# Bank layout, weight casts, squares and a rank step around the last attention pairs of a fused attention and expert kernel

## The chip, the cores and the metric

The kernel runs on one core of one Trainium2 chip. The metric is the device time of one execution in microseconds (us), the median of the runs shown. One execution was also recorded by the hardware profiler, and all rows come from it. PE is TensorE, PEld its weight load, ACT ScalarE, DVE VectorE, POOL GpSimd, SP SyncE.

## What is computed

A block-causal attention over 8 batches of 8 heads, 576 positions and 64 columns a head, followed by a mixture of experts on its output, where each token goes to the one expert that its normalised row fits best. Cut to its core, the reference reads:

```python
scores = np.where(mask, scale * q @ k.T, -1e9)           # mask: block_i >= block_j, blocks of 64
attn = np.exp(scores - scores.max(-1, keepdims=True))
x = attn / (attn.sum(-1, keepdims=True) + 1e-9) @ v      # (8, 8, 576, 64) -> 4608 rows of 512
xn, en = x / (norm(x) + 1e-6), emb / (norm(emb) + 1e-6)
logits = xn @ en.T / tau                                 # 8 experts
e = logits.argmax(1)
gate = softmax(logits)[arange(4608), e]
out = gate[:, None] * (np.maximum(x @ w1[e], 0) @ w2[e]) # w1: 512 x 1024, w2: 1024 x 512
```

## The kernel before, in words

The 8 batches of 8 heads make 32 pairs of heads, four pairs to a batch, numbered 0 to 31. Each pair goes through generators: prep, maxes, `scores` (L405; matmuls L422, exponentials on ScalarE L429 and L431 into pT and pA, adds on GpSimd L401 and L403 into pS), `values` (L441; matmuls L457, copies into oe L463), `sums` (L468; matmuls L476, L486, L493 to L500, copy into su L502) and `finish` (L514), which turns su and oe round on TensorE (L326), divides on VectorE into the token rows xrow (L532 to L545), and ends with the squares of the pair's columns on ScalarE (`parts_squares`, L562, one L582 of 128 columns for each of five row tiles). For pair 30 alone the squares aren't done there but put in a list `late`, which the tail runs.

Behind the last pair of a batch comes `route` (L587): the expert of each token on VectorE (L594 to L607), its rank among the tokens of that expert by matmuls (L616, L619, L620), the squares of whole rows (L582, 512 columns), the norm on GpSimd (L648, L651), the place of each token in a table (`table_rows`, L740: a product on GpSimd L745, then VectorE L747 to L752), the gate (L655 to L663), and five indirect DMAs of GpSimd that scatter the token numbers into the table (L672). In the same queue of slow steps stands `early_rows` with `indices` (L690; four small GpSimd operations on enone, L694 to L697), for the rows of two early slots.

The order of all this is written out by hand: one string of letters for each pair (`plan_of`), where s, v, f, m, p, l each run the next piece of scores, values with sums, finish, maxes, prep or loads, k a piece of the router's weights, and r the next piece of the slow queue. The last five pairs have strings of their own in FINAL; FINAL[3] is the string of pair 30, during which the steps of batch 6 go.

Behind the strings stands the tail (from L1240). It reads the token table into tbt (L1243), and starts the expert stage on two early slots of 128 tokens, whose rows ex are at hand before the last batch is routed. A weight of 32 bits is used as a high and a low piece in the rings ring_h (`split_hi`, a cast, L907) and ring_l (`split_lo`, a subtraction, L912); so are the rows, turned round on TensorE (`xt_turn`, L1093) into PSUM and split out of it (`xt_hi` L1097 on ScalarE into xh and hh, `xt_lo` L1101 on VectorE into xl and hl). The first expert layer (`l1`, L1309, by way of `mm3`, matmuls L1122) takes three matmuls for a weight piece and a half of its columns: high by high, low by high, high by low.

PSUM has eight banks. In the attention stage they are four pairs, psm0 (banks 0 and 1) to psm3 (6 and 7), which `take_bank` and `give_bank` hand round in a list. Before the tail the pair `free_bank` (psm2, banks 4 and 5) is taken out for the early rows' turned halves, one bank each. Then three pools take over the eight banks: ps_b (a pair), ps_m1 (four single banks) and ps_e (a pair), in the order in which they are opened; in the kernel before these are banks 0 and 1, 2 to 5, 6 and 7. The main expert stage has a pool `mps` of its own with rotating tiles ph, px, pt and py.

The code that fixes the banks and the casts:

```python
for c in range(NPC):
    split_hi(0, c, 0, eng=nc.gpsimd if c > 1 else nc.scalar)
    if c < 2:
        split_lo(0, c, 0)
load_raw(1, 0, eng=nc.gpsimd)
banks.remove(free_bank)
for u in range(EARLY):
    xt_turn(ea[u], free_bank[:, u])
```

Of the kernel before, what the change touches and what calls it, by code (L numbers as in the profile page):

```python
# [8 lines left out]
F32 = mybir.dt.float32  # L9
# [6 lines left out]
PSUM = bass.MemoryType.PSUM  # L16
# [15 lines left out]
    "rmmvrrvmvvvvrvvspvsrmpsrrrsrvfmvsvrrmrmfflsprrrfvvvrvmmrsfsffrrpvppsspvvppvmvssrrmrmvrvvmmrsmrsrmmsfrfsffssfprrrsmlvfprm",  # L32
    "srvmvpmmrvvrrvmrrrrvrrmppmmrrmvvrrrvvrrrrrmrrrrrrrlp",
    "slrvrrrrmrpsrprrsrsrspsrrrmmssrrrssrrrrrmssmmrmsrfrrfvvrvvrr",
    "rfvfsrrrmrrsmrfvfmrrrrsrrmsvmrvvrrvvrrsrrfrfrvfrrrsfvvfrsvvfvvrvrfrr",
    "rvrrvrrvvlrrrsfrffrrvvsrrrvrvrrrsrrfrsvvfsrfsfffvfrfvrrssrrfffrrrvss",
)

# [10 lines left out]
def kernel(  # L49
# [12 lines left out]
    nc = tc.nc  # L62
# [3 lines left out]
    P = 128  # L66
# [108 lines left out]
    NPAIR = B * NP  # L175
# [6 lines left out]
    def pool(stack, name, bufs, **kw):  # L182
        return stack.enter_context(tc.tile_pool(name=name, bufs=bufs, **kw))
# [10 lines left out]
    psum_t = psum.enter_context(ExitStack())  # L194
    ps_m = pool(psum_t, "ps_m", 1, space=PSUM)
    banks = [ps_m.tile([P, 2, 512], F32, name=f"psm{i}") for i in range(4)]
# [4 lines left out]
    def take_bank():  # L201
        return banks.pop(0) if wide else ps_b.tile([P, 2, 512], F32, name="psb")

    def flat2(t):
        return t.rearrange("p g c -> p (g c)")

    def give_bank(t):
        if wide:
            banks.append(t)
# [114 lines left out]
    def halves_turned(out, a):  # L324
        for g in range(2):
            nc.tensor.transpose(out(g), a[hd[g]], ident[hd[g], hd[g]])  # L326
# [187 lines left out]
    def finish(n, xrow, rin, lgh, ssp):  # L514

        hp = n % NP
        tb = take_bank()
        pt = flat2(tb)

        yield "pe"  # L520
        u0, u1 = NJ * 64, NJ * 64 + 64
        for u in range(2):
            halves_turned(lambda g: pt[:, g * 512 + u0 + u * 64:g * 512 + u0 + u * 64 + 64], su[n % 2][:, u * P:(u + 1) * P])
        yield "fine"
        for j in range(NJ - 1, -1, -1):
            halves_turned(lambda g: pt[:, g * 512 + j * 64:g * 512 + j * 64 + 64], oe[n % len(oe)][:, j * P:(j + 1) * P])
        yield
        r2 = rin[:, :, 2 * hp:2 * hp + 2]
        p2 = pt.rearrange("p (a x) -> p a x", a=2)
        lt = p2[:, :, u0:u1].rearrange("p a (j c) -> p a j c", c=32)  # L530
        c1, c2 = u1 + 32 + 2 * E, 512 + u1 + 2 * E + 1
        nc.vector.tensor_scalar(r2[:, 0:NG].rearrange("p (a j) c -> p a j c", a=2), lt[:, :, :, 2 * E:2 * E + 2],  # L532
                                1.0e-9, None, op0=ALU.add)
        nc.vector.tensor_scalar(r2[:, NG], pt[:, c1:c2 + 1:c2 - c1], 1.0e-9, None, op0=ALU.add)
        nc.vector.reciprocal(r2, r2)
        yield "fine"
        xp = xrow[:, :, hp * P:(hp + 1) * P].rearrange("p j (g d) -> p j g d", d=D)
        nc.vector.tensor_tensor(xp, p2[:, :, 0:u0].rearrange("p g (j d) -> p j g d", d=D),
                                r2.unsqueeze(3).to_broadcast((P, NJ, 2, D)), op=ALU.mult)
        yield  # L540
        for a in range(2):
            nc.vector.tensor_tensor(lgh[:, 2 * a:2 * a + 2, 2 * hp:2 * hp + 2, :],
                                    lt[:, a, :, 0:2 * E].rearrange("p j (g e) -> p j g e", e=E),
                                    r2[:, 2 * a:2 * a + 2].unsqueeze(3).to_broadcast((P, 2, 2, E)), op=ALU.mult)
        nc.vector.tensor_tensor(lgh[:, NG, 2 * hp:2 * hp + 2, :],  # L545
                                pt[:, u1:u1 + 2 * E].rearrange("p (g e) -> p g e", e=E),
                                r2[:, NG].unsqueeze(2).to_broadcast((P, 2, E)), op=ALU.mult)
        give_bank(tb)
        yield
        if n == NPAIR - 2:  # L550
            store(B - 1, xrow, 0, (NP - 1) * P)
        if n >= NPAIR - NP:
            yield "squares"
            if n == NPAIR - 2:
                late.append(lambda: parts_squares(hp, xrow, ssp))
            else:
                parts_squares(hp, xrow, ssp)
            yield

    late = []  # L560

    def parts_squares(hp, xrow, ssp):  # L562
        for j in range(NJ):
            squares(xrow[:, j, hp * P:(hp + 1) * P], ssp[:, j, hp:hp + 1])

    def store(b, xrow, c0, c1):
        r0 = b * S + 1
        nc.sync.dma_start(xbuf[r0:r0 + S - 64, c0:c1].rearrange("(j p) w -> p j w", p=P), xrow[:, 0:NJ - 1, c0:c1])
        nc.sync.dma_start(xbuf[r0 + S - 64:r0 + S, c0:c1], xrow[0:64, NJ - 1, c0:c1])
# [331 lines left out]
    def piece(ring, i, c, half):  # L901
        cs = slice(c * CW, (c + 1) * CW)
        return ring[i][:, half, cs] if isinstance(half, int) else flat(ring[i][:, bass.ds(half, 1), cs])

    def split_hi(i, c, half, to=None, eng=nc.scalar):
        to = i if to is None else to
        return (nc.scalar.copy if eng is nc.scalar else eng.tensor_copy)(  # L907
            piece(ring_h, to, c, half), raw[i][:, c * CW:(c + 1) * CW])

    def split_lo(i, c, half, to=None, eng=nc.vector):  # L910
        to = i if to is None else to
        return eng.tensor_tensor(piece(ring_l, to, c, half), raw[i][:, c * CW:(c + 1) * CW],  # L912
                                       piece(ring_h, to, c, half).bitcast(F32), op=ALU.subtract)
# [104 lines left out]
    def rotate(pool, name, n, shape, dt):  # L1018
        sets[name] = [pool.tile(shape, dt, name=f"{name}{i}") for i in range(n)]
        turn[name] = 0  # L1020
# [234 lines left out]
        slots[g]["w", 0] = half_of(0, 0)  # L1255
        slots[g]["w", 1] = half_of(0, 1)
    for c in range(NPC):
        split_hi(0, c, 0, eng=nc.gpsimd if c > 1 else nc.scalar)
        if c < 2:
            split_lo(0, c, 0)  # L1260
    load_raw(1, 0, eng=nc.gpsimd)
    banks.remove(free_bank)
    for u in range(EARLY):
        xt_turn(ea[u], free_bank[:, u])
    drain(values(NPAIR - 1))
# [4 lines left out]
    split_lo(0, 2, 0)  # L1270
    xt_lo(ea[1], free_bank[:, 1])
    psum_t.close()
    ps_b = pool(psum_t, "ps_b", 1, space=PSUM, reuse_waits="tile")
    ps_m = pool(psum_t, "ps_m1", 4, space=PSUM, reuse_waits="tile")
    wide.clear()
    ps_e = pool(psum_t, "ps_e", 1, space=PSUM, reuse_waits="tile")
    pts = [ps_e.tile([P, 512], F32, name=f"pe{u}") for u in range(2)]
    drain(last_f)
    split_lo(0, 3, 0)
    late.pop()()  # L1280
    for c in range(NPC):
        split_hi(1, c, 1, to=0, eng=nc.gpsimd)
    load_raw(0, 1, (2, 3, 0, 1))
# [103 lines left out]


    mps = ctx.enter_context(tc.tile_pool(name="mps", bufs=1, space=PSUM, reuse_waits="tile"))
    rotate(mps, "py", 1, [P, DM], F32)  # L1390
    rotate(mps, "px", 1, [P, 512], F32)
    rotate(mps, "ph", 2, [P, 512], F32)
    rotate(mps, "pt", 2, [P, 1024], F32)
    NU = NT // P - EARLY

    def turn_pe(g):
# [130 lines left out]
```

## Time and profile before

| what | value |
|---|---|
| runs | 811.25, 808.84, 810.61 us |
| median | 810.61 us |
| the profiled execution | 810.42 us |
| its span, from the first instruction to the last | 808.7 us |
| granted TensorE clock, mean | 1.0 |
| TensorE, busy share of the span | 96% |
| VectorE, GpSimd, ScalarE | 75%, 54%, 50% |
| DMA over the span | 93.95 MB, 116 GB/s |

The attention stage and the change's place end near 363 us; from there on TensorE runs expert matmuls of 512 columns to the end. A timeline row gives the start of an instruction (or of several alike, counted after the x) and its duration in us, engine, line and operation, the tiles written and read, and in brackets how long the engine stood idle ahead of it and what released it. A "q" behind an engine's name is its instruction queue or sequencer.

### The profile page before, as it was taken

How to read it: one execution, taken by the hardware profiler on the slowest of the kernel's cores; microseconds unless marked ns; L12 is line 12 of the kernel's file. 1: busy time of each engine (PE TensorE's matmuls, PEld its weight loads, DVE VectorE, ACT ScalarE, POOL GpSimd, SP SyncE). 2: the span in 40 equal slices, each digit the busy share in tenths (PEclk: the TensorE clock that was granted, in tenths of full speed). 3: DMA queues.
4: the chain of work that ended last, by engine and by line, in shares of the span. 5: the costliest groups of instructions: out<-in, count | busy, mean ns of one | idle time of the engine just before them, and what ended most of it. 6: DMA issues, size and time to landing. Idle time of an engine off the chain costs nothing. (4 is left out here: it accounts for less than half of the span.)

```text
span 808.7 us, 23043 instructions
## 1 busy us (share of the span) xinstructions
PE 779.2 (96%) x7160; PEld 627.3 (78%) x7160; DVE 604.2 (75%) x1382; ACT 408.4 (50%) x831; POOL 435.7 (54%) x420
## 2 busy tenths in 40 slices
PE   8999999999999998899999999999999999999997
PEld 3678878787878776668878887788888888888885
DVE  6667878686868776658868777877887778877881
ACT  2566757575757564664744456553533332543222
POOL 7555676767676757772347288784761111661110
PEclk9999999999999999999999999999999999999999
DMA  4745364545454543163845357454441111111111
GB/s 104 169 95 136 84 158 105 147 104 132 101 140 100 141 100 101 29 231 127 297 151 166 100 158 235 152 167 150 148 153 45 55 54 45 38 49 55 54 35 39
DMA packets 141421, 93.95 MB, mean 116 GB/s; under 512 B 118925, under 2 KB 120541, under 8 KB 141260
## 3 DMA queue, kind: packets, MB, share of 16 engines
q1 hardware_dynamic: 133228, 69.74, 31.2%
q0 software_dynamic: 8032, 22.36, 8.7%
q8 instruction: 66, 1.08, 0.6%
q14 instruction: 95, 0.78, 0.3%
HBM read 72.71 MB, written 19.71 MB: 114 GB/s over the span
## 5 line engine op out<-in xcount | busy, mean ns | idle before, releaser
L1175 DVE STREAM_TRANSPOSE pt<-h 32x256 f32<-32x256 f32 x528 | 240.6, 456 | 31.3 <-ACT h L1149 14.1
L367 DVE TENSOR_REDUCE nmx<-psm 128x16 f32<-128x1024 f32 (+2 forms) x128 | 125.6, 986 | 21.4 <-PE psm L361 18.5
L912 POOL TENSOR_TENSOR ring_l<-raw,ring_h 128x1024 f32 (+1 forms) x49 | 116.3, 2406 | 35.7 <-ACT ring_h L907 20.0
L1189 POOL DMA_INDIRECT out_dram<-y,outi x36 | 36.7, 1020 | 176.5 <-ACTq L1061 118.8
L1122 PE MATMUL py<-ring_h,hh 128*128 x272 | 109.3, 402 | 0.7 <-ACT h L1149 0.7
L1122 PE MATMUL py<-ring_l,hh 128*128 x272 | 106.3, 391 | 0.0
L429 ACT ACTIVATE pT<-psm 128x640 f32<-128x640 f32 (+2 forms) x128 | 89.1, 703 | 28.2 <-PE psm L361 16.8
L403 POOL TENSOR_TENSOR pS<-pS,pT 128x640 f32<-128x640 f32 (+2 forms) x93 | 93.5, 1006 | 10.9 <-ACT pT L431 3.2
L1122 PE MATMUL py<-ring_h,hl 128*128 x272 | 88.8, 389 | 0.0
L1122 PE MATMUL ph<-ring_l,xh 128*128 x280 | 86.3, 390 | 0.8 <-POOLq L1073 0.8
L1122 PE MATMUL ph<-ring_h,xh 128*128 x280 | 86.3, 389 | 0.6 <-ACTq L1061 0.6
L457 PE MATMUL psm<-pT,vo 128*64 128x320 f32 (+2 forms) x640 | 76.1, 380 | 1.0 <-issue 1.0
L1188 ACT ACTIVATE y<-py,xg 128x512 f32<-128x512 f32 x34 | 23.4, 689 | 103.5 <-PE py L1122 97.9
L1183 DVE TENSOR_TENSOR hl<-pt,hh 128x512 fp32r<-128x512 f32 x66 | 42.5, 686 | 42.0 <-ACT hh L1181 42.0
L422 PE MATMUL psm<-qh,kh 64*128 64x320 f32 (+4 forms) x384 | 66.5, 341 | 5.9 <-ACT pT L429 3.5
L907 ACT CAST ring_h<-raw 128x1024 f32 (+1 forms) x62 | 61.0, 1050 | 22.1 <-POOLq L1073 11.6
L1181 ACT CAST hh<-pt 128x512 fp32r<-128x512 f32 x66 | 35.5, 590 | 72.1 <-DVE pt L1175 71.7
L1122 PE MATMUL ph<-ring_h,xl 128*128 x280 | 69.2, 389 | 0.0
L457 PEld LDWEIGHTS psm<-pT,vo 128*64 128x64 f32 x640 | 43.2, 137 | 29.3 <-issue 1.9
L1122 PEld LDWEIGHTS ph<-ring_l,xh 128*128 128x128 f32 x280 | 52.5, 188 | 12.1 <-POOLq L1073 1.2
L1122 PEld LDWEIGHTS ph<-ring_h,xh 128*128 128x128 f32 x280 | 52.5, 188 | 11.7 <-ACTq L1061 0.8
L1122 PEld LDWEIGHTS ph<-ring_h,xl 128*128 128x128 f32 x280 | 52.6, 188 | 10.9
(289 smaller groups left out, 1680.7 us busy)
## 6 DMA issues: line engine op xcount, KB each, us to landing
raw<-in_moe_w_dram SPq DMA_DIRECT2D x60, 512.0 KB
qn<-in_q_dram SPq DMA_DIRECT2D x64, 128.0 KB
kn<-in_k_dram SPq DMA_DIRECT2D x64, 128.0 KB
vo<-in_v_dram SPq DMA_DIRECT2D x64, 128.0 KB
xbuf<-xrow SPq DMA_DIRECT2D x28, 260.0 KB
raw<-in_moe_w_dram POOLq DMA_DIRECT2D x4, 512.0 KB
qa<-nmT SPq DMA_DIRECT2D x64, 2.5 KB
xbuf<-xrow SPq DMA_DIRECT2D x7, 130.0 KB
```

The source lines that it names most:

```text
L367: nc.vector.tensor_reduce(m[:, :, f:f + o // w], mt[:, :, 0:o].rearrange("p h (b c) -> p h b c", c=w), axis=AX.X, op=ALU.max, negate=True)
L403: nc.gpsimd.tensor_tensor(o, o, pT[:, :, off[t]:off[t] + w], op=ALU.add)
L422: nc.tensor.matmul(st[0:kw, hh, o:o + c1 - c0], kk[hd[hh], t * P:t * P + kw], qq[hd[hh], 64 + c0:64 + c1], start=(x == 0), stop=(x == len( ...
L429: nc.scalar.activation(pT[:, :, f:f + w] if c0 else pA, st[:, :, 0:w], AF.Exp, scale=scale)
L457: m = nc.tensor.matmul(ob[hh * D:(hh + 1) * D, b0:b0 + q1 - c0], rows(vo, ends_v, n, t)[:, hh, :], pTs[hh][0][:, f0:f0 + q1 - c0] if c0 el ...
L907: return (nc.scalar.copy if eng is nc.scalar else eng.tensor_copy)(piece(ring_h, to, c, half), raw[i][:, c * CW:(c + 1) * CW])
L912: return eng.tensor_tensor(piece(ring_l, to, c, half), raw[i][:, c * CW:(c + 1) * CW], piece(ring_h, to, c, half).bitcast(F32), op=ALU.sub ...
L1122: m = nc.tensor.matmul(out, ac, slots[g]["w", i](r, c * n + off), start=(u == 0 and c == 0), stop=(c == nk - 1 and u == len(turns) - 1))
L1175: nc.vector.transpose(pt[32 * j:32 * j + 32, :, 32 * i:32 * i + 32], h[32 * i:32 * i + 32, :, j, :])
L1181: nc.scalar.copy(sets["hh"][u], pt[:, 4 * u:4 * u + 4])
L1183: nc.vector.tensor_tensor(sets["hl"][u], pt[:, 4 * u:4 * u + 4], sets["hh"][u].bitcast(F32), op=ALU.subtract)
L1189: nc.gpsimd.indirect_dma_start(out=out, out_offset=bass.IndirectOffsetOnAxis(ap=to, axis=0), in_=y, in_offset=None, bounds_check=NT - 1, o ...
```

## The change

It has four parts.

- In the string of pair 30 four letters r are taken out, so that each later piece of batch 6's routing runs some letters later.
- The squares of pair 29 join those of pair 30 in the list `late`, which the tail now runs through as a whole.
- The first four high weight pieces are cast by ScalarE (1 and 3) and GpSimd (0 and 2) in turn, where ScalarE had 0 and 1, GpSimd 2 and 3.
- The order of the remaining bank pairs is turned round behind the first, so that sums of pair 31 take psm3 in place of psm0, and the pools are opened in the order ps_m1, ps_e, ps_b: banks 0 to 3, 4 and 5, 6 and 7. The main pool's tiles are declared in the order ph, px, pt, py.

```diff
 FINAL[3]
-    "rfvfsrrrmrrsmrfvfmrrrrsrrmsvmrvvrrvvrrsrrfrfrvfrrrsfvvfrsvvfvvrvrfrr",
+    "rfvfsrrrmrrsmrfvfmrrrrsrrmsvmrvvvvsrrfrfrvfrrrsfvvfrsvvfvvrvrfrr",
...
 finish
-            if n == NPAIR - 2:
+            if NPAIR - 4 < n < NPAIR - 1:
                 late.append(lambda: parts_squares(hp, xrow, ssp))
...
     for c in range(NPC):
-        split_hi(0, c, 0, eng=nc.gpsimd if c > 1 else nc.scalar)
+        split_hi(0, c, 0, eng=nc.scalar if c % 2 else nc.gpsimd)
...
     banks.remove(free_bank)
+    banks[1:] = banks[:0:-1]
...
     psum_t.close()
+    ps_m = pool(psum_t, "ps_m1", 4, space=PSUM, reuse_waits="tile")
+    ps_e = pool(psum_t, "ps_e", 1, space=PSUM, reuse_waits="tile")
     ps_b = pool(psum_t, "ps_b", 1, space=PSUM, reuse_waits="tile")
-    ps_m = pool(psum_t, "ps_m1", 4, space=PSUM, reuse_waits="tile")
     wide.clear()
-    ps_e = pool(psum_t, "ps_e", 1, space=PSUM, reuse_waits="tile")
...
-    late.pop()()
+    for f in late:
+        f()
...
+    rotate(mps, "ph", 2, [P, 512], F32)
+    rotate(mps, "px", 1, [P, 512], F32)
+    rotate(mps, "pt", 2, [P, 1024], F32)
     rotate(mps, "py", 1, [P, DM], F32)
-    rotate(mps, "px", 1, [P, 512], F32)
-    rotate(mps, "ph", 2, [P, 512], F32)
-    rotate(mps, "pt", 2, [P, 1024], F32)
```

What the string does is seen in the order of the instructions. On TensorE, at the rank matmuls of batch 6 during pair 30 (pT_212 and vo_159 belong to pair 29's values, hot_109 to the ranks), the rows run:

```order
 L457 MATMUL psm_150<-pT_212,vo_159 64x320 x6
+L457 MATMUL psm_150<-pT_212,vo_159 64x192 x2
+L457 MATMUL psm_150<-pT_212,ve_167 64x64 x2
 L616 LDWEIGHTS triS
 L616 MATMUL psm_153<-hot_109,triS 128x40
```

Between these rows and the next stand the other rank matmuls, unchanged; behind them:

```order
 L620 LDWEIGHTS onesb
 L620 MATMUL psm_153<-hot_109,onesb 128x40
-L457 MATMUL psm_150<-pT_212,vo_159 64x192 x2
-L457 MATMUL psm_150<-pT_212,ve_167 64x64 x2
 L326 MATMUL psm_151<-ident,su_205 128x64 x4
```

The last four value matmuls of pair 29 (two rows of two) now stand ahead of the rank matmuls. On GpSimd, some time behind, at the product and the scatters of the same batch:

```order
 L651 TENSOR_SCALAR ss<-ss,half 128x5
-L745 TENSOR_TENSOR t_5973<-t_5973,hot_109 128x40
 L403 TENSOR_TENSOR pS<-pS,pT_211 128x2x192
 L403 TENSOR_TENSOR pS<-pS,pT_211 128x2x64
+L745 TENSOR_TENSOR t_5979<-t_5979,hot_109 128x40
 L657 TENSOR_TENSOR lg<-lg,ss 128x40
-L672 DMA table<-tokf,rowj 36864x1 x3
 L694 TENSOR_SCALAR enone<-et 128x2
 L695 TENSOR_TENSOR enone<-et,enone 128x2
 L696 TENSOR_SCALAR enone<-enone 128x2
 L697 CAST ei<-enone 128x2
-L672 DMA table<-tokf,rowj 36864x1 x2
+L672 DMA table<-tokf,rowj 36864x1 x5
```

The product goes behind two adds, and the three scatters that stood ahead of the enone operations go behind them. On TensorE, at the early rows' transposes and the first expert matmuls, with the waits that each row has (the names number engines and DMA queues):

```order
-L1093 MATMUL psm_152<-ident,ex_216 128x128 [waits DMASW0_49,DVE_49]
+L422 MATMUL psm_152<-qh_184,kh_190 128x192 [waits DVE_49]
+L422 MATMUL psm_152<-qh_184,kh_190 128x192
+L422 MATMUL psm_152<-ql_187,kh_190 128x192 x2
+L422 MATMUL psm_152<-qh_184,kl_193 128x192 x2
+L422 MATMUL psm_152<-qa_196,ka 128x192 x2
+L422 MATMUL psm_152<-qh_184,kh_190 64x64 x2
+L422 MATMUL psm_152<-ql_187,kh_190 64x64 x2
+L422 MATMUL psm_152<-qh_184,kl_193 64x64 x2
+L422 MATMUL psm_152<-qa_196,ka 64x64 x2
+L1093 MATMUL psm_152<-ident,ex_216 128x128 [waits DMASW0_49,Activation_49]
```

Pair 31's last scores now write the transposes' own bank pair. A little later the first six expert matmuls stood so:

```order
-L1122 MATMUL psm<-ring_h_6260,xh_6268 128x512 [waits PE_49,Activation_49]
-L1122 MATMUL psm<-ring_l_6261,xh_6268 128x512 [waits DVE_49]
-L1122 MATMUL psm<-ring_h_6260,xl_6269 128x512 [waits DVE_49]
-L1122 MATMUL psm<-ring_h_6260,xh_6268 128x512 [waits DVE_49]
-L1122 MATMUL psm<-ring_l_6261,xh_6268 128x512
-L1122 MATMUL psm<-ring_h_6260,xl_6269 128x512
```

The fourth waits for VectorE there. In the changed kernel they stand so:

```order
+L1122 MATMUL psm<-ring_h_6250,xh_6258 128x512 [waits Activation_49,Pool_49]
+L1122 MATMUL psm<-ring_l_6251,xh_6258 128x512 [waits DVE_49]
+L1122 MATMUL psm<-ring_h_6250,xl_6259 128x512 [waits DVE_49]
+L1122 MATMUL psm<-ring_h_6250,xh_6258 128x512 [waits PE_49]
+L1122 MATMUL psm<-ring_l_6251,xh_6258 128x512
+L1122 MATMUL psm<-ring_h_6250,xl_6259 128x512
```

The transposes wait for ScalarE (Activation) where they waited for VectorE; and the fourth expert matmul for TensorE itself where it waited for VectorE.

## Rows read from the trace of the kernel before

**Rows 1.** Part 1 of the page: busy us of each engine, share, instructions.
```profile
PE 779.2 (96%) x7160; PEld 627.3 (78%) x7160; DVE 604.2 (75%) x1382; ACT 408.4 (50%) x831; POOL 435.7 (54%) x420
```
**Rows 2.** Timeline of TensorE, 337 to 364 us: start, us, instruction, [idle before <-releaser].
```profile
338.05 0.19 PE L616 MATMUL psm<-hot,triS 128*128 128x40 bf16 x1 [0.93 <-DVE hot L607]
...
338.30 0.55 PE L457 MATMUL psm<-pT,vo 128*64 128x192 f32 x4
...
338.89 0.34 PE L326 MATMUL psm<-ident,su 64*128 64x64 f32 x4
...
346.02 0.76 PE L493 MATMUL psm<-oe,enT 128*32 128x128 f32 x6 [0.36 <-ACT oe L463]
...
351.47 0.23 PE L422 MATMUL psm<-qa,ka 64*64 64x64 f32 x2
352.05 1.09 PE L1093 MATMUL psm<-ident,ex 128*128 128x128 f32 x8 [0.35 <-issue]
...
358.86 0.40 PE L1122 MATMUL psm<-ring_h,xl 128*128 128x512 f32 x1
360.05 0.50 PE L1122 MATMUL psm<-ring_h,xh 128*128 128x512 f32 x1 [0.79 <-DVE hl L1101]
360.39 0.39 PE L1122 MATMUL psm<-ring_l,xh 128*128 128x512 f32 x1
360.62 0.40 PE L1122 MATMUL psm<-ring_h,xl 128*128 128x512 f32 x1
...
362.91 0.53 PE L1333 MATMUL psm<-ident,tbt 128*96 128x128 f32 x3
```
**Rows 3.** The same timeline later: first and last of three waits.
```profile
407.70 0.72 PE L1122 MATMUL ph<-ring_h,xh 128*128 x2 [0.58 <-ACTq L1061]
...
506.47 0.66 PE L1093 MATMUL px<-ident,xg 128*128 128x128 f32 x4 [1.08 <-DMA xg<-xbuf,rowi]
```
**Rows 4.** Timeline of ScalarE, 335 to 365 us.
```profile
346.00 0.41 ACT L463 COPY oe<-psm 128x320 f32<-128x320 f32 x1
...
350.05 0.31 ACT L582 ACTIVATE xs<-xrow 128x128 f32<-128x128 f32 x1
...
352.09 1.87 ACT L429 ACTIVATE pT<-psm 128x896 f32<-128x896 f32 x3
353.84 0.27 ACT L431 ACTIVATE pT<-psm 64x128 f32<-64x128 f32 x1
...
364.86 0.60 ACT L1315 ACTIVATE h<-psm 128x512 f32<-128x512 f32 x1 [4.09 <-PE psm L1122]
```
**Rows 5.** Timeline of VectorE, 335 to 365 us.
```profile
351.83 0.17 DVE L545 TENSOR_TENSOR lgh<-psm,rin 128x16 f32<-128x16 f32 x1
...
359.31 0.69 DVE L1101 TENSOR_TENSOR hl<-psm,hh 128x512 fp32r<-128x512 f32 x1
```
**Rows 6.** Timeline of GpSimd, 335 to 365 us.
```profile
341.64 1.54 POOL L403 TENSOR_TENSOR pS<-pS,pT 128x384 f32<-128x384 f32 x2
...
344.76 1.10 POOL L672 DMA_INDIRECT table<-tokf,rowj  x1 [0.50 <-issue]
...
351.50 0.97 POOL L672 DMA_INDIRECT table<-tokf,rowj  x1 [0.30 <-issue]
...
355.10 2.96 POOL L169 DMA_DIRECT2D raw<-in_moe_w_dram  x4
359.19 1.11 POOL L907 CAST ring_h<-raw 128x1024 fp32r<-128x1024 f32 x1 [1.12 <-DMA raw<-in_moe_w_dram]
```
**Rows 7.** Timeline of SyncE's DMA queue, 335 to 365 us.
```profile
346.64 1.97 SPq L576 DMA_DIRECT2D xbuf<-xrow  x4
...
356.38 0.33 SPq L1243 DMA_DIRECT2D tbt<-table  x1
```
**Rows 8.** Timeline of TensorE: 448-column scores of an earlier pair and of pair 31.
```profile
325.89 0.37 PE L422 MATMUL psm<-qa,ka 64*128 64x448 f32 x2
...
348.65 0.88 PE L422 MATMUL psm<-qa,ka 64*128 64x448 f32 x2
```

## The prediction

> **What bounds the kernel now.** I read the engine shares first: TensorE is busy 96% of the span [rows 1], so a change pays only where TensorE stands still, or by taking work from it, and this one takes none. Next I went through TensorE's own timeline for rows with an idle time in brackets. In the stretch that the change touches (the last attention pairs and the first expert matmuls) there are four [rows 2]: 0.93 us ahead of the rank matmuls L616, 0.36 ahead of the sums L493, 0.35 ahead of the early rows' transposes L1093, and 0.79 ahead of the fourth expert matmul L1122. Together they are 2.43 us, 0.3% of the run: the most that this change can win from the waits which the view marks. There are three waits behind that, the first and the last of which are [rows 3]; they are ruled by weight casts and gathers whose loops TensorE's own progress releases, so what is won ahead of them should come through to the end.
>
> The timelines of the other engines say who ends each of the four. L616 waits for VectorE's hot rows, as its bracket says. L493 waits for ScalarE's copy of oe, which starts at 346.00 and ends at 346.41 [rows 4]. L1093 is put down to "issue", but TensorE's rows hold nothing there, and VectorE's last read of the bank pair that the transposes write (L545 of pair 30) ends at 351.83 + 0.17 = 352.00 [rows 5], 0.05 before they start. L1122 waits for hl, VectorE's L1101, which ends at 359.31 + 0.69 = 360.00 [rows 5]: the fourth matmul doesn't read hl; hl is read out of the second bank of the pair that held the transposes, and the matmul's own output tile lies in that bank.
>
> **The change, part by part.**
>
> *Bank layout.* The first expert matmuls now write banks 0 and 3, the transposes stay in 4 and 5, and the order rows show the wait on VectorE gone from the fourth matmul, with a wait on TensorE itself in its place. Without it the fourth follows the third at the pace of its neighbours, 360.62 - 360.39 = 0.23 us [rows 2]: the fourth starts at 358.86 + 0.23 = 359.09 and the fifth at 359.32, where it started at 360.39. That is **-1.07 us** (0.79 of idle time and the refill behind it). Bounds: 0 if another operand is late there, -1.07 if none is. The fourth reads the other half of the weight piece that the three before it read, so I take -1.07.
>
> *Squares of pair 29.* Five squares leave ScalarE ahead of the exponentials of pair 31. They ran from 350.05 to where the exponentials begin, 352.09 [rows 4]: 2.04 us. The exponentials took 353.84 + 0.27 - 352.09 = 2.02 us, and can now run as the scores come. The last scores start at 351.47 and take 0.23 [rows 2], and two short exponentials are left behind them (about 0.5 us of the 2.02), so they should end at about 352.3 instead of 354.11. This matters because of the banks: the order rows show that the transposes now wait for ScalarE, whose exponentials read the last scores out of banks 4 and 5, and no longer for VectorE. So L1093 goes from 352.05 to between 352.2 and 352.5, and I take 352.4, **+0.35 us**. The five squares join five others, ahead of the first relu, which stood idle for 4.09 us waiting for TensorE until 364.86 [rows 4]. They take 2.04 of it, and the gain about 1 more: hidden, with 1.0 us to spare; without that cover each 0.41 us of a square would be paid.
>
> *Rank step of batch 6.* The last value matmuls of pair 29, from 338.30 to 338.89, now stand ahead of L616 and fill 0.59 of its 0.93 of idle time [rows 2]. That isn't 0.59 on the path, for TensorE stops again at 346.02 for oe. That copy stands behind a small exponential (gx) on ScalarE's queue, which needs GpSimd's product t x hot and VectorE's row arithmetic. The product is put behind two adds, 1.54 us together [rows 6], while VectorE's finish of pair 29 goes ahead of the row arithmetic, which lets ScalarE's squares start sooner than now. Going through the four queues with the durations of today I get the copy at about 345.75 instead of 346.00: **-0.25 us**. Bounds: -0.95 (both waits filled) and +0.95 (the two adds wholly on the path, 1.54, less the 0.59).
>
> *The table.* This is the same step's other end. The five scatters of the token table (L672) began at 344.76; the last starts at 351.50 and ends at 352.47 [rows 6]. The product comes about 2.1 us later (the two adds, and some 0.6, most of it a copy of oe, 0.41 long, that ScalarE now does ahead of three squares). Against that stand four small GpSimd operations between the third scatter and the fourth. A scatter and the gap ahead of it take 0.97 + 0.30 = 1.27, four of them 5.1, and from the first to the last it was 351.50 - 344.76 = 6.7: so those operations held up the scatters by 1.6 us. They now run ahead of all five, while the rows are still being made. I put the last scatter's end at 353.5, **1.0 later**, with 0.5 (2.1 less 1.6) and 2.1 as bounds. SyncE's read of the table into tbt was issued 356.38 - 352.47 = 3.9 us behind it [rows 7], so it goes to 357.4. How long it takes to land no row shows. The nearest row is a weight piece that GpSimd asked for at 355.10 and whose cast, waiting for it, began at 359.19 [rows 6]: 4.1 us. At the most it is 362.91 - 356.38 = 6.5 us, as L1333 started at 362.91 without a wait [rows 2]. With 4.1 the table is there at 361.5, and TensorE gets to L1333 at 362.91 - 0.97 = 361.94: just hidden, and 0.4 us from being the next bound. I cost it at **0**.
>
> *Casts.* ScalarE and GpSimd swap pieces 0 and 2 against 1 and 3 as they stand; four casts stay four, and the first expert matmul starts behind the sums of pair 31, not behind a cast. **0**: the first expert matmul stands behind the sums of pair 31 and showed no wait for a cast; were that cover gone, GpSimd's first piece would be late by what the scatters are, 1.0. The main pool's banks are in another order as well, with no wait that ends last: 0.
>
> **Sum**: -1.07 + 0.35 - 0.25 = -0.97, and I round the rank step's small gain off a little: about **-0.9 us**. The profiled execution took 810.42 us (a span of 808.7 and 1.7 around it); 809.5 in its place. The median of the runs is 0.19 above it, so **809.7 us**. A measurement of this kernel can tell about 0.3% from no change, 2.4 us; this is no change.
>
> At one place a rule speaks against the change. The trace shows the transposes released by VectorE at 352.00 while ScalarE's exponentials ran on until 354.11 [rows 4, 5], in another bank pair, so that they cost TensorE nothing there. The Trainium skill (Perfetto Trace Analysis, Optimizing Tensor Performance, Matmuls) says that independent groups of matmuls should rotate through different PSUM banks, so that one group's eviction overlaps the next group's matmuls. By that rule the layout is worse for the transposes than it was; left in a free pair they would make the sum -1.3, and the second rival is the rule at its worst.
>
> **Rivals.**
>
> *The slow stretch goes too (faster).* Between 347.6 and 349.5 the scores of 448 columns take 0.88 us a pair, in two of their four forms, where they took 0.37 with an earlier pair [rows 8]: 1.0 us in all, and no wait is marked. It falls behind the stores of the attention rows, issued from 346.64 on [rows 7]. If the moved queues pull the scores away from these, up to 1.0 more is won, though the table then holds L1333 at about 361.5, so that the whole is 1.4, or 1.97 if the table lands quicker: 808.6 to 809.2 us. Against it: nothing in the change moves the stores, and the scores move by 0.25 only.
>
> *The transposes wait for the old exponentials (slower).* If ScalarE doesn't use the time that the squares leave, because the exponentials are held by something that I don't see, L431 still ends at 354.11 and the transposes start 2.06 us later than now. With the gain of 1.07 and 0.25 that is +0.75, **811.4 us** against the median of 810.61. It decides as soon as L431 ends later than 352.05 + 1.32 = 353.4. For it speaks that the wait is really there in the new order; against it, that the bracket ahead of those exponentials names nothing but the squares.
>
> *The table is late (slower).* The same step with 6.5 us for tbt: it lands at 363.9, TensorE waits for 1.9, the sum is +1.0, 811.6 us. It decides from a landing time of 4.5 us on; the row that is nearest says 4.1.
>
> *Nothing happens.* The hl wait stays, because another operand is late as well, and the small terms cancel: 810.6 us.
>
> **How the numbers follow.** My forecast (-0.4 to -1.3) has 0.50; the slow stretch going as well, 0.18; the transposes or the table late, 0.17 together; nothing, 0.15. The range takes in all four with the bounds of the rank step, less the ends: 807.9 to 811.8. All of it lies within 0.3% of 810.61 but for the lowest part: faster by over 0.3% (below 808.2) needs the slow stretch, the rank step's best bound and a quick table together, or something that no row here shows; I give that 0.15. Slower by over 0.3% (above 813.0) needs two late things at once: 0.07. Same: 0.78.
>
> **What would show it.** In the changed profile the bracket of 0.79 at the fourth L1122 should be gone, and the first twelve of these evenly 0.23 apart. The transposes should start within 0.2 us behind the end of L431, at about 352.4. L616 should show some 0.3 instead of 0.93, and L493 still a small wait for oe. L1333 should show no wait for tbt, or one below 0.5. I'm wrong if L1093 starts behind 353.4, if L1333 waits more than 1 us, or if the three later waits grow by what was won ahead of them.

## The result, and the profile after

The changed kernel takes **813.77 us** (median of 7 runs, 811.66 to 816.46), the kernel before 809.82 (median of 7 runs of the same comparison): a ratio of **1.0051, 95% interval 1.0030 to 1.0072**. It is slower by about 4 us where 0.9 less was forecast, and above the range that was given (807.9 to 811.8). Its profiled execution took 813.49 us, with a span of 811.8 against 808.7. TensorE's busy time hardly moved (779.2 us before [rows 1]); it stood still for longer. The engines' shares on the page of the changed kernel, as in [rows 1]:

```profile
PE 780.1 (96%) x7160; PEld 629.8 (78%) x7160; DVE 604.6 (74%) x1382; ACT 409.3 (50%) x831; POOL 437.7 (54%) x420
```

TensorE's timeline shows where. The columns are those of [rows 2]:

```profile
332.79 0.30 PE L361 MATMUL psm<-kh,qh 64*128 64x64 f32 x2
...
337.76 0.19 PE L616 MATMUL psm<-hot,triS 128*128 128x40 bf16 x1 [0.50 <-ACT oe L463]
...
344.60 0.80 PE L493 MATMUL psm<-oe,enT 128*32 128x128 f32 x6
...
346.85 0.37 PE L422 MATMUL psm<-qa,ka 64*128 64x448 f32 x2
...
347.17 0.48 PE L326 MATMUL psm<-ident,oe 64*128 64x64 f32 x10
...
347.97 0.31 PE L422 MATMUL psm<-qa,ka 64*128 64x320 f32 x2
...
348.69 0.22 PE L422 MATMUL psm<-qa,ka 64*64 64x64 f32 x2
354.14 1.97 PE L1093 MATMUL psm<-ident,ex 128*128 128x128 f32 x8 [5.22 <-ACT pT L431]
...
362.11 0.50 PE L1122 MATMUL psm<-ring_h,xh 128*128 128x512 f32 x1
...
362.69 0.40 PE L1122 MATMUL psm<-ring_h,xl 128*128 128x512 f32 x1
362.92 0.40 PE L1122 MATMUL psm<-ring_h,xh 128*128 128x512 f32 x1
...
365.67 0.53 PE L1335 MATMUL psm<-ident,tbt 128*96 128x128 f32 x3
```

What the prediction looked for ahead of the transposes is there, and more. L616 waits 0.50 instead of 0.93, L493 waits no longer, the 448-column scores take 0.37 instead of 0.88 [rows 8], and the fourth expert matmul follows the third by 0.23, without its 0.79 [rows 2]. TensorE is through with the last scores at 348.69 + 0.22 = 348.91, and then it stands still for **5.22 us**, until ScalarE's last exponential ends. ScalarE was not busy in that time. Its timeline, where [rows 4] had three exponentials of L429 in one piece, from 352.09:

```profile
346.45 1.73 ACT L429 ACTIVATE pT<-psm 128x640 f32<-128x640 f32 x2 [0.45 <-PE psm L422]
350.49 0.70 ACT L429 ACTIVATE pT<-psm 128x640 f32<-128x640 f32 x1 [2.32 <-remote]
353.44 0.49 ACT L429 ACTIVATE pT<-psm 128x384 f32<-128x384 f32 x1 [2.24 <-remote]
353.83 0.26 ACT L431 ACTIVATE pT<-psm 64x128 f32<-64x128 f32 x1
```

The scores of 320 columns end at 347.97 + 0.31 = 348.28, and their exponential starts at 350.49; the last scores end at 348.91, and theirs starts at 353.44. In the program's order the first of the two waits for TensorE alone; the second waits for a read of VectorE's too, which had ended before 347. VectorE's row arithmetic (L532) is late in the same way: it reads what L326 had written by 347.17 + 0.48 = 347.65, and starts at 349.10 on VectorE's timeline:

```profile
349.10 0.17 DVE L532 TENSOR_SCALAR rin<-psm 128x8 f32<-128x8 f32 x1 [2.41 <-PE psm L422]
...
349.62 0.82 DVE L538 TENSOR_TENSOR xrow<-psm,rin 128x640 f32<-128x640 f32 x1
```

The brackets name no engine ("remote"), or the last of TensorE's rows. VectorE's own signal is not late: its division ends at 349.62 + 0.82 = 350.44, and the store that waits for it goes out at 350.47, by the timeline of SyncE's queue (the last line answers to the table's read in [rows 7]):

```profile
350.47 0.38 SPq L568 DMA_DIRECT2D xbuf<-xrow  x1
...
354.80 0.33 SPq L1243 DMA_DIRECT2D tbt<-table  x1
```

So it is what waits for TensorE that comes late in these rows: by 1.45, 2.2 and 4.5 us. In just that time GpSimd issues the five scatters of the token table, one behind the other, where [rows 6] had them from 344.76 on with other operations between; its timeline:

```profile
346.23 1.11 POOL L672 DMA_INDIRECT table<-tokf,rowj  x1 [0.58 <-issue]
347.65 0.99 POOL L672 DMA_INDIRECT table<-tokf,rowj  x1 [0.30 <-issue]
348.94 0.98 POOL L672 DMA_INDIRECT table<-tokf,rowj  x1 [0.30 <-issue]
350.23 0.97 POOL L672 DMA_INDIRECT table<-tokf,rowj  x1 [0.31 <-issue]
351.50 0.97 POOL L672 DMA_INDIRECT table<-tokf,rowj  x1 [0.30 <-issue]
353.43 2.02 POOL L907 CAST ring_h<-raw 128x1024 fp32r<-128x1024 f32 x2 [0.95 <-remote]
```

The cast in the last row is late too: in the program's order it waits for all but the last two matmuls of pair 31's scores, which had ended by 348.9, and for loads that had landed earlier, and it starts at 353.43, with ScalarE's exponential. What the rows can't tell is whether the signals came late or the matmuls ended later than shown, for the profile models where a matmul ends; "late signals" stands here for both. The matmuls that follow do start at their usual pace, up to the last at 348.69.

The standstill has a second price. The view of the stretches (columns: from and to, length, busy us and instructions of TensorE's matmuls, its weight loads, VectorE, ScalarE and GpSimd, then TensorE's granted clock as a share, the DMA share and GB/s) shows the granted clock at one half, 1.2 instead of 2.4 GHz, from 351.0 on, after TensorE had stood still since 348.9, and back at full speed only at 357.8, though it had been at work again since 354.14:

```profile
348.00:351.00 3.00, 0.91 (x20) 0.80 (x18) 1.55 (x7) 0.68 (x2) 2.39 (x3) 1.00 0.52 160
351.00:354.00 3.00, 0.00 (x0) 0.00 (x0) 0.00 (x0) 0.76 (x4) 1.75 (x3) 0.50 0.85 287
354.00:357.80 3.80, 3.66 (x18) 2.77 (x20) 3.16 (x2) 2.14 (x4) 3.80 (x6) 0.50 0.36 81
357.80:362.00 4.20, 4.20 (x92) 3.39 (x88) 0.71 (x2) 1.61 (x4) 1.60 (x2) 1.00 1.01 388
```

The eight transposes take 1.97 us instead of 1.09. From their start to the first expert matmul it is 362.11 - 354.14 = 7.97 us, where it was 358.29 - 352.05 = 6.24.

Two rows of TensorE's timeline before, which this reading and the next need beside [rows 2]:

```profile
333.08 0.30 PE L361 MATMUL psm<-kh,qh 64*128 64x64 f32 x2
...
358.29 0.50 PE L1122 MATMUL psm<-ring_h,xh 128*128 128x512 f32 x1
```

**The sum of the stretch.** The runs' starts differ: the last score maxima (two matmuls L361 of 64 columns) begin at 333.08 us in the profile of before, at 332.79 in that of after. From them to the turn of the token table (L1333, in the changed kernel L1335) it is 362.91 - 333.08 = 29.83 us before and 365.67 - 332.79 = 32.88 after: **+3.05**, the whole difference of the spans. It is made up of -2.50 (the last scores end sooner), +4.87 (idle time of 5.22 instead of 0.35), +1.73 (the clock) and -1.06 (the bank layout). What lies behind the stretch took 445.8 us before and 446.1 after.

### The profile page after: what moved, and what is told of

It is laid out like the page before. It is cut to its first block, busy times and chain, and to the rows that moved or that the text cites. A ratio compares the mean times of both kernels' runs of the same rounds, so it can differ in the third digit from the quotient of the medians.

```text
span 811.8 us, 23041 instructions
## 1 busy us (share of the span) xinstructions
PE 780.1 (96%) x7160; PEld 629.8 (78%) x7160; DVE 604.6 (74%) x1382; ACT 409.3 (50%) x831; POOL 437.7 (54%) x420
## 5 line engine op out<-in xcount | busy, mean ns | idle before, releaser
L367 DVE TENSOR_REDUCE nmx<-psm 128x16 f32<-128x1024 f32 (+2 forms) x128 | 125.6, 986 | 21.4 <-PE psm L361 18.7
L429 ACT ACTIVATE pT<-psm 128x640 f32<-128x640 f32 (+2 forms) x128 | 89.3, 703 | 32.3 <-PE psm L361 16.9
L907 ACT CAST ring_h<-raw 128x1024 f32 (+1 forms) x62 | 60.9, 1049 | 21.8 <-issue 10.7
L422 PE MATMUL psm<-qh,kh 64*128 64x320 f32 (+4 forms) x384 | 66.5, 342 | 5.5 <-ACT pT L429 3.4
```

The costliest lines, as they stand in the source:

```text
L367: nc.vector.tensor_reduce(m[:, :, f:f + o // w], mt[:, :, 0:o].rearrange("p h (b c) -> p h b c", c=w), axis=AX.X, op=ALU.max, negate=True)
L422: nc.tensor.matmul(st[0:kw, hh, o:o + c1 - c0], kk[hd[hh], t * P:t * P + kw], qq[hd[hh], 64 + c0:64 + c1], start=(x == 0), stop=(x == len( ...
L429: nc.scalar.activation(pT[:, :, f:f + w] if c0 else pA, st[:, :, 0:w], AF.Exp, scale=scale)
```

## The experiments

All experiments are read by this stretch, because single profiled executions differ by several us ahead of it: in one of them, with the same instructions up to there, it began at 336.86 instead of 331.57. Each row gives the start of the last L361, of the table's turn, the difference, the idle time ahead of the early rows' transposes (L1093), and the end of the last exponential (L431) behind that L361.

| kernel | last L361 | table's turn | stretch | idle ahead of L1093 | L431 ends |
|---|---|---|---|---|---|
| before | 333.08 | 362.91 | 29.83 | 0.35 | 21.0 |
| after | 332.79 | 365.67 | 32.88 | 5.22 | 21.3 |
| string back | 331.57 | 360.25 | 28.68 | 0.34 | 20.6 |
| string only | 331.79 | 368.03 | 36.24 | 5.76 | 21.8 |
| turned into the other pair | 331.92 | 360.48 | 28.56 | 1.84 | 21.3 |
| banks and casts only | 336.86 | 365.54 | 28.68 | 0.34 | 20.9 |
| both stores late | 334.56 | 367.05 | 32.49 | 5.19 | 21.3 |
| store of batch 7 late | 333.65 | 366.77 | 33.12 | 5.28 | 21.4 |
| no scatters of batch 6 | 333.26 | 359.89 | 26.63 | 0.74 | 16.8 |
| two scatters of five | 336.53 | 363.95 | 27.42 | 1.52 | 17.6 |
| before, no scatters of batch 6 | 332.45 | 360.94 | 28.49 | 0.52 | 19.4 |
| other pair, both stores late | 333.12 | 361.69 | 28.57 | 1.14 | 21.3 |
| other pair, scatters sooner | 333.75 | 367.40 | 33.65 | 1.56 | 20.9 |

### Which part of the change

**The string put back**, all else as in the changed kernel.

```diff
-    "rfvfsrrrmrrsmrfvfmrrrrsrrmsvmrvvvvsrrfrfrvfrrrsfvvfrsvvfvvrvrfrr",
+    "rfvfsrrrmrrsmrfvfmrrrrsrrmsvmrvvrrvvrrsrrfrfrvfrrrsfvvfrsvvfvvrvrfrr",
```

> The changed kernel with the string of pair 30 as it was before; banks, squares and casts stay changed. Theory A (TensorE pays because the string exchanged two bank pairs, so that the turned early rows go to the pair which ScalarE's last exponentials still read, and those end near 354.1 because TensorE's signals reach ScalarE late): with the old string the transposes wait for VectorE again, the 5.2 us of idle time ahead of L1093 is gone or below 1, and the time is 1 to 2 us below the kernel before, about 808.5. Theory B (the squares' move idles ScalarE and TensorE's clock falls for it): the wait stays above 3 us and the time near 813.5.

Measured: 810.15 us, ratio to before 1.0001 (0.9985 to 1.0016); stretch 28.68, idle time 0.34. The wait is gone, as Theory A says. The time is that of before and not the 1 to 2 us less that was expected: the gain of 1.15 us in the stretch is 0.14%, less than the interval can tell.

**The string alone**, put into the kernel before.

```diff
-    "rfvfsrrrmrrsmrfvfmrrrrsrrmsvmrvvrrvvrrsrrfrfrvfrrrsfvvfrsvvfvvrvrfrr",
+    "rfvfsrrrmrrsmrfvfmrrrrsrrmsvmrvvvvsrrfrfrvfrrrsfvvfrsvvfvvrvrfrr",
```

> The kernel before with the new string of pair 30 alone. Theory A: the transposes wait for the last exponentials, which end near 354, so L1093 starts near 354 as in the changed kernel, with 3 to 5 us idle ahead of it, and the time is 3 to 5 us above the kernel before (813 to 815). Theory B: the squares still stand on ScalarE, nothing idles, the time is that of the kernel before within 1 us.

Measured: 815.90 us (four runs), ratio 1.0071 (1.0044 to 1.0099), 0.9 above the range that was expected. TensorE's timeline has the wait and the slow transposes, and the wait for hl, which the bank layout would have taken away, at the fourth expert matmul:

```profile
353.67 1.97 PE L1093 MATMUL psm<-ident,ex 128*128 128x128 f32 x8 [5.76 <-ACT pT L431]
...
362.94 0.50 PE L1122 MATMUL psm<-ring_h,xh 128*128 128x512 f32 x1
...
365.19 0.50 PE L1122 MATMUL psm<-ring_h,xh 128*128 128x512 f32 x1 [1.28 <-DVE hl L1101]
```

The string costs 36.24 - 29.83 = 6.4 us of the stretch on its own. Of this 3.0 lie between the start of the transposes and the first expert matmul, where it is 362.94 - 353.67 = 9.27 us instead of 6.24: TensorE was at half clock for longer than in the changed kernel. Theory B falls: the squares stand where they stood, and TensorE waits all the same.

**The early rows turned into the other pair.**

```diff
-    free_bank = banks[2]
+    free_bank = banks[3]
```

> The changed kernel with the early rows turned into the other pair (psm3 instead of psm2), which VectorE leaves near 350.7; all else as in the changed kernel. Theory A: L1093 starts by 351, the values of pair 31 still wait for the exponentials that end near 354.1, and the time falls by 3 to 4 us from the changed kernel, to 809 to 811. If the late signals alone set the end, by less than 1.5.

Measured: 810.38 us, ratio 1.0002 (0.9987 to 1.0018); stretch 28.56, 4.3 less than in the changed kernel. The transposes wait for VectorE for 1.84 us, and the exponentials are just as late as in the changed kernel, but now the transposes and the first values run beside them, and the granted clock stays at 1.00 up to the table's turn. TensorE's timeline:

```profile
349.88 1.09 PE L1093 MATMUL psm<-ident,ex 128*128 128x128 f32 x8 [1.84 <-DVE xrow L538]
...
360.48 0.53 PE L1335 MATMUL psm<-ident,tbt 128*96 128x128 f32 x3
```

ScalarE's timeline of the same kernel:

```profile
349.60 0.71 ACT L429 ACTIVATE pT<-psm 128x640 f32<-128x640 f32 x1 [2.30 <-remote]
352.52 0.49 ACT L429 ACTIVATE pT<-psm 128x384 f32<-128x384 f32 x1 [2.21 <-PE psm L457]
```

So two things come together in the changed kernel: the late signals, and a bank pair that makes TensorE wait for their consumer. The string exchanged the pairs psm2 and psm3 in the order rows; by the program that is because the rank matmuls take their pair later in the list, and the string alone has the wait: the new bank layout of the tail has no part in it.

**Bank layout and casts alone**, in the kernel before (in the changed kernel the string and the squares put back).

```diff
-            if NPAIR - 4 < n < NPAIR - 1:
+            if n == NPAIR - 2:
...
-    "rfvfsrrrmrrsmrfvfmrrrrsrrmsvmrvvvvsrrfrfrvfrrrsfvvfrsvvfvvrvrfrr",
+    "rfvfsrrrmrrsmrfvfmrrrrsrrmsvmrvvrrvvrrsrrfrfrvfrrrsfvvfrsvvfvvrvrfrr",
```

> The kernel before with the bank layout and the order of casts of the changed one; string and squares as before. Both theories: the 0.79 us ahead of the fourth L1122 is gone, and the time is about 1.0 us below the kernel before (0.12%).

Measured: 809.78 us, ratio 0.9989 (0.9974 to 1.0004), stretch 28.68: -1.15 us. With the squares moved as well (the string put back, above) the stretch is the same 28.68: beside the old string the squares' move is worth nothing. ScalarE's timeline of that run shows why:

```profile
349.89 0.70 ACT L429 ACTIVATE pT<-psm 128x640 f32<-128x640 f32 x1 [0.50 <-PE psm L422]
351.51 0.49 ACT L429 ACTIVATE pT<-psm 128x384 f32<-128x384 f32 x1 [0.92 <-PE psm L422]
```

The five squares are out of the way, and the exponentials wait all the same: the last scores end at 350.12, and theirs starts 1.39 behind. They end 20.6 us behind the last L361 instead of 20.9, 0.35 sooner, where the prediction had 1.8 for this. Beside the new string no run measures the squares' move by itself. The stretches of single executions leave 32.88 - (36.24 - 1.15) = -2.2 us for it, 1.3 of this from the transposes to the first expert matmul (9.27 against 7.97).

### What holds the signals up

Two suspects lie in that time: the bursts of stores of the token rows, and the token table's scatters. First the stores, moved behind the read of the table (in the second run the first store of batch 7 alone):

```diff
-            store(B - 1, xrow, 0, (NP - 1) * P)
+            held.append(lambda: store(B - 1, xrow, 0, (NP - 1) * P))
...
-                if (b == B - 2 or j == NJ - 1) and pieces:
+                if b < B - 2 and j == NJ - 1 and pieces:
...
     for f in late:
         f()
+    while pieces:
+        store_piece()
+    for f in held:
+        f()
```

> The changed kernel with the stores of the last two batches' rows (L576, L578 of batch 6 and L568, L569 of batch 7) held back to the tail, behind the read of the token table; scatters where they were. Theory A1 (TensorE's signals are late because they come during the bursts of these stores): ScalarE's exponentials follow the scores, L431 ends by 350.5 instead of 354.1, the idle time ahead of L1093 falls from 5.2 to below 2 us, and the stretch from the last L361 to L1335 falls from 32.9 to below 30 us. Theory A2 (the token table's scatters hold the signals up): no change, 5 us of idle time.

> The changed kernel with the first store of batch 7 (L568, L569) alone held back to the tail; the five stores of batch 6 stay at 345 to 348 us. Theory A1: the last signal, which came 4.5 us late during this store's burst, comes about 2 us earlier, and L1093 starts near 351.5 with 2 to 3.5 us of idle time. Theory A2: 5 us of idle time as before.

Measured: 814.73 and 814.68 us (one execution each; the kernel before had a median of 810.62 on that chip), idle times of 5.19 and 5.28. With all seven stores out of the way (the first goes out at 355.81) ScalarE's two waits are what they were, 2.28 and 2.24, by its timeline of the run with both stores late:

```profile
352.23 0.70 ACT L429 ACTIVATE pT<-psm 128x640 f32<-128x640 f32 x1 [2.28 <-remote]
355.18 0.49 ACT L429 ACTIVATE pT<-psm 128x384 f32<-128x384 f32 x1 [2.24 <-remote]
```

Its SyncE queue, with the read of the table ahead of the stores:

```profile
355.36 0.33 SPq L1243 DMA_DIRECT2D tbt<-table  x1
355.81 2.04 SPq L576 DMA_DIRECT2D xbuf<-xrow  x4
```

Theory A1 falls. Then the scatters, left out for batch 6:

```diff
-                w = nc.gpsimd.indirect_dma_start(
+                w = b < B - 2 and nc.gpsimd.indirect_dma_start(
```

> The changed kernel without the token table's scatters of batch 6 (the five L672): that batch's tokens are not put into the table and go to no slot, and nothing else is left out. Theory A2: ScalarE's exponentials follow the scores, L431 ends by 350.5, the idle time ahead of L1093 is below 2 us. Theory A1: the stores' bursts are as they were, L431 still ends near 353 to 354, and the idle time stays above 4 us.

Measured: 807.54 us (one execution, beside the same 810.62), stretch 26.63. The exponentials run without a gap behind the scores, the last one ends 16.8 us behind the last L361 instead of 21.3, and TensorE waits 0.74. ScalarE's timeline:

```profile
346.92 3.00 ACT L429 ACTIVATE pT<-psm 128x640 f32<-128x640 f32 x4 [0.46 <-PE psm L422]
349.81 0.26 ACT L431 ACTIVATE pT<-psm 64x128 f32<-64x128 f32 x1
```

VectorE's row arithmetic starts 0.12 us behind what it reads (348.11), where that was 1.45, although the stores of batch 6 go out in that time, from 345.74 to 348.28. VectorE's timeline:

```profile
348.23 0.17 DVE L532 TENSOR_SCALAR rin<-psm 128x8 f32<-128x8 f32 x1 [1.08 <-PE psm L326]
```

TensorE's:

```profile
350.12 1.09 PE L1094 MATMUL psm<-ident,ex 128*128 128x128 f32 x8 [0.74 <-ACT pT L431]
...
359.89 0.53 PE L1336 MATMUL psm<-ident,tbt 128*96 128x128 f32 x3
```

This is what the prediction had expected of the changed kernel. So it is the scatters. How much a part of them costs:

```diff
-                w = nc.gpsimd.indirect_dma_start(
+                w = (b < B - 2 or j < 2) and nc.gpsimd.indirect_dma_start(
```

> The changed kernel with two of batch 6's five scatters left (the other three tiles' tokens don't get into the table). If the scatters hold TensorE's signals up for as long as GpSimd issues them (Theory A2), signals come about 0.8 us behind the end of the second, 16.4 to 16.7 us behind the last L361: the scores of pair 31 end at 16.1, L431 ends near 17.3 (21.3 with five, 16.8 with none), and the idle time ahead of L1093 is 1.0 to 1.5. If a single scatter were enough to hold them for 4 us, L431 would still end near 21.

Measured: 812.0 us (one execution, with other differences ahead of the stretch), stretch 27.42, L431 ends 17.6 us behind the last L361, idle time 1.52. With none, two and five scatters it ends at 16.8, 17.6 and 21.3. VectorE's row arithmetic is as late with two as with five: it starts 352.87 - 336.53 = 16.3 us behind the last L361, as in the changed kernel (349.10 - 332.79), and 1.49 behind what it reads (351.38). Its timeline:

```profile
352.87 0.17 DVE L532 TENSOR_SCALAR rin<-psm 128x8 f32<-128x8 f32 x1 [2.45 <-PE psm L422]
```

So two scatters are enough to make a signal late by 1.5 us, and more of them hold the later ones. In the changed kernel the last of the late exponentials starts at 353.44, 0.97 behind the end of the last scatter (351.50 + 0.97). The kernel before, by this reading, should pay as well, in another place; there the scatters of batch 6 are left out in the same way:

```diff
-                w = nc.gpsimd.indirect_dma_start(
+                w = b < B - 2 and nc.gpsimd.indirect_dma_start(
```

> The kernel before without the five scatters of batch 6 (its tokens don't get into the table). A2 says that the kernel before pays as well: the 2.3 us that ScalarE's copy of su stood idle and the slow scores of 448 columns go, and the stretch from the last L361 to the table's turn falls from 29.8 by 1 to 2 us. If the slow scores come from the stores: the stretch stays within 0.4 us.

Measured: 808.34 us (one execution; the kernel before had a median of 811.53 on that chip), stretch 28.49, 1.34 less than before. ScalarE's copy of su starts without the 2.3 us of idle time that it had (in the kernel before it is put down to L422, although the sums that it copies had been written 2.3 us earlier). ScalarE's timeline of the kernel before:

```profile
349.24 0.32 ACT L502 COPY su<-psm 128x192 f32<-128x192 f32 x1 [2.32 <-PE psm L422]
```

The same without the scatters:

```profile
346.40 0.32 ACT L502 COPY su<-psm 128x192 f32<-128x192 f32 x1
```

And its 448-column scores, which took 0.88 [rows 8], on TensorE's timeline:

```profile
347.58 0.37 PE L422 MATMUL psm<-qa,ka 64*128 64x448 f32 x2
```

### In search of a faster version

Two were run, both with the early rows turned into the other pair. In the first the stores are held back as well (with the other lines of that edit, above):

```diff
-    free_bank = banks[2]
+    free_bank = banks[3]
...
-            store(B - 1, xrow, 0, (NP - 1) * P)
+            held.append(lambda: store(B - 1, xrow, 0, (NP - 1) * P))
```

> The early rows turned into psm3 and both stores held back to the tail, the rest as in the changed kernel: the version that would beat both if Theory A1 holds. A1: nothing waits for a late signal, the stretch from the last L361 to L1335 falls from 29.8 (before) and 28.6 (other pair alone) to about 26, and the time to 806.5 to 808, unless the late stores delay the table or the weights. A2: as with the other pair alone, 810.

Measured: 810.20 us, ratio 0.9998 (0.9981 to 1.0015), stretch 28.57. Nothing is won, as A2 says. In the second the scatters go sooner, in one row behind the gate's exponent and ahead of the four enone operations:

```diff
         nc.scalar.activation(gx[b % 2][:, :, 0:E], lg, AF.Exp)
         yield
+        if b == B - 2:
+            yield from scatter(b, rowj, False)
...
-            for j in range(NJ):
-                w = nc.gpsimd.indirect_dma_start(
...
+            if b < B - 2:
+                yield from scatter(b, rowj, True)
+            else:
+                while pieces:
+                    store_piece()
...
-        if n > NPAIR - NP - 2 and early_g:
+        if NPAIR - NP - 2 < n < NPAIR - 1 and early_g:
```

> The early rows turned into psm3 (as with the other pair), and the five scatters in one row right behind the gate's exponent, ahead of the four enone operations: they start about 12 us and end about 18 us behind the last L361 instead of 13.4 and 19.7. A2: the last exponentials end 1.0 to 1.6 us sooner (about 20 instead of 21.25), the stretch to L1335 falls from 28.6 to 27.2 to 28.0, and the time to 0.2 to 0.35% below the kernel before; if TensorE's earlier signals get late in exchange, the stretch stays near 28.6.

Measured: 815.22 us, ratio 1.0036 (1.0007 to 1.0066), stretch 33.65. A miss: slower, where 0.2 to 0.35% less was expected. The scatters now meet the scores of pair 31 while TensorE still waits for ScalarE and VectorE in between, so that TensorE itself stands still in several places, and its transposes take 1.97 us again. Its timeline:

```profile
350.29 0.42 PE L422 MATMUL psm<-qh,kh 64*128 64x320 f32 x2 [1.24 <-ACT pT L429]
...
352.46 0.19 PE L422 MATMUL psm<-ql,kh 64*64 64x64 f32 x1 [0.46 <-issue]
353.19 0.25 PE L422 MATMUL psm<-qh,kl 64*64 64x64 f32 x2 [0.54 <-issue]
...
355.06 1.97 PE L1102 MATMUL psm<-ident,ex 128*128 128x128 f32 x8 [1.56 <-DVE lgh L545]
```

No version was found that measures faster than the kernel before. By the stretch the best that computes everything is 28.56, 1.3 us below it. The 26.63 without scatters are no version, for tokens are missing; they say what a place for the scatters would be worth where nobody waits for TensorE.

## Why the prediction was wrong

- **Bank layout, -1.07: right.** 4.62 us from the first expert matmul to the table's turn before, 365.67 - 362.11 = 3.56 after: -1.06. Alone, with the casts, -1.15.
- **Casts, 0, and table, 0: right in the sum.** L1335 shows no wait. The last scatter ended at 351.50 + 0.97 = 352.47 and not at 353.5, and the table was asked for at 354.80, 2.3 behind it instead of 3.9.
- **Rank step, -0.25: right in the mechanism that was named, but not worth anything.** L616's wait fell to 0.50 and L493's went. TensorE ended the last scores 2.5 us sooner, beyond even the best bound of 0.95, because the copy of su (345.67) got through ahead of the scatters (from 346.23) and the 448-column scores ran at 0.37, neither of which was in this step's reckoning. All of it was lost at the next wait.
- **Squares, +0.35: the step that failed.** The exponentials "can now run as the scores come", so that they should end at about 352.3 and the transposes start 0.35 later. They ended at 353.83 + 0.26 = 354.09, as before the change (354.11), though ScalarE was idle for 4.6 us between them, and the transposes started 2.09 later. The step took the squares for what held the exponentials, because the row of before has no bracket; behind the squares stood TensorE's signals, late by the scatters, which the squares' time had covered. With the squares moved beside the old string, 0.35 of the 1.8 us came; without scatters the step comes out as it was written. The sum also had no term for TensorE's clock, which fell in the standstill: +1.73.
- **What the second rival had, and lacked.** Its mechanism came true, with the old end of L431 and the transposes released by it. Its price of 0.75 lacked the clock (1.73), and it took off the rank step's 0.25, which a wait at a fixed time swallows. 354.14 - 352.05 = 2.09 (2.38 by the stretch), +1.73, -1.06 give the 3.05. Its chance was low for the reason that "the bracket ahead of those exponentials names nothing but the squares". There is no bracket in that row, and none would have told: a bracket shows the wait that ended last, not those that it covers.
- **The first rival** (the slow scores go as well) came true too, but not by the stores: they were slow because of the scatters, as the run without them shows.
- **The string's part** was not seen: the prediction knew that the transposes would wait in the exponentials' bank pair, and laid it to "the banks" and "the layout"; it was the four letters that exchanged the pairs. The bank layout alone has no such wait (28.68, 0.34 idle). The Trainium skill (Perfetto Trace Analysis, Optimizing Tensor Performance, Matmuls) wants independent groups of matmuls to rotate through different PSUM banks, so that an eviction overlaps with the next group. The trace agrees: with the same late exponentials the stretch is 32.88 in the bank pair that they read and 28.56 in the other.

## What to carry to other kernels

An engine's busy stretch ahead of a late instruction may cover a second wait; before counting on it to move up, check when its operands' signals were used by somebody else, or try it without the cover. Where banks are handed round in a list, a step moved by some letters exchanges them for all that follow, so look up, for each tile that is reused, which engine leaves it last. A long standstill of TensorE can be charged twice, with its length and with the time at half clock behind it (here 5.2 and 1.7 us; the 1.84 us with the other pair left the clock at 1.00).

## What was not expected of the hardware

While GpSimd issues the indirect DMAs that scatter the token table, what waits for TensorE on ScalarE, VectorE and GpSimd comes late in these runs: by up to 4.5 us with five in a row, by up to 1.5 with two, by no more than 0.12 on VectorE with none; VectorE's signal to SyncE went out at once in the same time. The stores do nothing of the kind: held back, they leave the waits as they are, and without scatters they run and nothing is late. What couples TensorE to the scatters no run shows, neither whether it is GpSimd's issuing or the transfers that it starts; the runs with none and with two are single executions, and it wasn't tried whether other indirect DMAs (the gathers and the output rows in the expert stage) do the same. By the program's steps the same scatters stand in every batch.
